# POOL issues later loads, and eight early heads make their scores from split parts

## The chip, the core and the metric

The kernel runs on one core of a Trainium2 chip. The metric is the device time of one execution in microseconds (us): the median of three runs was 1068.83 us, the lowest 1068.21 and the highest 1069.07. The engines are called as in the profile: PE multiplies matrices (PEld is its loading of weights), DVE and ACT work on whole tiles element by element, POOL did little before, and SP only issues transfers.

## What is computed

Eight batches with eight heads of attention over 512 local and 32 global positions, and then a feed-forward layer over all 8 x 544 tokens:

```python
k_all = np.concatenate([k_g, k_l], axis=2)
v_all = np.concatenate([v_g, v_l], axis=2)
s_g = scale * np.matmul(q_g, k_all.transpose(0, 1, 3, 2))
out_g = np.matmul(sm(s_g), v_all)                      # global queries see every key
s_ll = scale * np.matmul(q_l, k_l.transpose(0, 1, 3, 2))
mask = np.abs(pos[:, None] - pos[None, :]) <= 32       # local queries see a band
s_ll = np.where(mask, s_ll, -1000000000.0)
s_lg = scale * np.matmul(q_l, k_g.transpose(0, 1, 3, 2))
a_l = sm(np.concatenate([s_lg, s_ll], axis=-1))
out_l = np.matmul(a_l, np.concatenate([v_g, v_l], axis=2))
x = concat([out_g, out_l], axis=2) as (8*544, 512)
h = np.maximum(x @ w_in, 0.0)                          # (512, 2048)
out = h * h @ w_out                                    # (2048, 512)
```

All inputs and outputs are float32. `sm` is a softmax over the last axis.

## The kernel before

The attention is cut into 128 head slots, `t` = 0 to 127: one head with one half (256) of its local queries. Sixteen slots hold one batch. A slot's keys, queries and values lie in one packed tile `raw` of 128 x 864 (columns 0 to 351 keys, 352 to 607 queries, the rest values), and keys and queries stand there twice, in partitions 0 to 63 and 64 to 127. The feed-forward layer works on blocks of 256 tokens; a block takes eight steps `m`, each with 256 of the 2048 inner columns. One program loop has a step `t` for every slot, and in it the feed-forward step `m = t - 9` (`LAG`).

Precision is bought in two ways. The first sixteen slots (`plain`, `NPLAIN` = 16) multiply float32 tiles as they are, and with keys and queries there twice their scores come out twice as large (`scale` is 0.0625 then). Every later slot is split (`split_head`, lines 125 to 137): ACT copies `raw` into `hi` in the format fp32r, DVE subtracts to get the rest, `lo`, and in the lower half of `hi` the keys are replaced by their own rests. `scores` (line 139) then makes each half of a slot's scores from two products, `hi` with `hi` and `lo` with `hi`, instead of one float32 product. The global queries' scores, `g_scores` (line 287), run against `qz`, a zeroed float32 tile that POOL fills for plain slots (lines 273 to 278), or against `qgz`, which holds the split queries, for the others; four slots share one. `g_evac` (line 301) takes the sums `gs` to `sg`: for split slots it is a copy on ACT and an addition on DVE.

Around this run the softmax (`softmax1` on DVE, `softmax2` on ACT, `softmax3` on DVE or ACT), the transposes of the probabilities into `pt`, their copy `pts` by ACT, the product with the values into `xa`, and its copy by ACT into `xg` or `x_h`. The weights come as 32 chunks `wr`, which ACT (`w_abs`) and DVE (`w_bits`, two operations) turn into float32 chunks `wf` for the first block; one such turn of a chunk is called a decode below. Later ACT and DVE make the split chunks `ws` from them (`w_chunk`). The table `PLAN` says at which of four places of step `t` a half decode (`b`) or a split (`s`) is written; what the table leaves out is made when it is needed (`w_need`).

For steps before 17 (`FREE`) the order of each engine's instructions is set by a scheduler from its own estimates; from step 17 on PE, DVE and ACT keep the order in which the program is written. All loads and stores but the first global query stand in SP's queue.

Of the kernel before, what the change touches and what calls it, by code (L numbers as in the profile page):

```python
# [16 lines left out]
P = 128  # L17
# [10 lines left out]
NPLAIN = 16  # L28

PLAN = [",,,b", "b,,,b", "b,,,b", "b,,b,", "b,,b,", "b,,b,", "b,,b,", "b,b,,b", "b,b,,b", "bb,bb,bb,bb", "bb,bb,bb,bb", "bbs,bb,bbs,bbs", "bbs,bbs,bbs,bbs", "bbs,bbs,bbs,bbs", "bbs,bbs,bs,s", "ss,s,s,s", "ss,s,s,s", "s,,s,", "s,,s,", "s,,s,", "s,,s,", "s,,s,", "s,,s,"]  # L30
# [28 lines left out]
def attention_moe(  # L59
# [10 lines left out]
    pe, ve, ac = InOrder(tc, nc.tensor), InOrder(tc, nc.vector), InOrder(tc, nc.scalar)  # L70
    PSUM = bass.MemoryType.PSUM
# [18 lines left out]
    def load_head(t):  # L90
# [5 lines left out]
        if t == 0:  # L96
            nc.sync.dma_start(raw[:, : QC + KC], pk[t, :, : QC + KC])
        else:
            nc.sync.dma_start(raw, pk[t])
# [165 lines left out]
    def g_load(t):  # L265
# [7 lines left out]
        if plain(t):  # L273
            qz = p1.tile([P, 512], F32, tag=("ph", "gvl", "gvh", "ph")[t // 4], name=f"qz{t}")
            nc.gpsimd.memset(qz, 0.0)
            qr = p1.tile([P, 2, 2, 32], F32, tag="qr", name=f"qr{t}")
            (nc.sync if t else nc.scalar).dma_start(qr, src)
            nc.gpsimd.tensor_copy(cols(qz, 0), qr)
# [8 lines left out]
    def g_scores(t):  # L287
# [4 lines left out]
        kk = hd["raw" if plain(t) else "hi"]  # L292
# [35 lines left out]
    def g_soft(t):  # L328
# [260 lines left out]
    for t in range(NSTEP + LAG + 1):  # L589
# [40 lines left out]
        if early and t + 1 < NPLAIN:  # L630
            scores(t + 1)
# [11 lines left out]
        if t + 1 < NT:  # L643
            split_head(t + 1)
# [126 lines left out]
```

## Time and profile before

| | before |
|---|---|
| median of 3 runs | 1068.83 us |
| the profiled execution's own time | 1068.82 us |
| its span | 1067.0 us |
| busy: PE, DVE, ACT, POOL | 1050.4, 856.3, 753.1, 3.9 us |
| granted clock of PE | 1.00 |
| DMA, read and written | 86.51 and 8.91 MB |

The span is what the instructions take from the first to the last; 1.8 us lie around it. Rows of the timeline give the start, the length and the engine of a group of equal instructions, and in brackets the idle time before it with what ended it. Rows of the stretches give, after the bounds and the length, the busy time of PE, PEld, DVE, ACT and POOL with the number of instructions in brackets, the granted clock, the share of the DMA engines and GB/s. Rows of the groups end with the total busy time and the mean length of one instruction in ns.

### The profile page before, as it was taken

Reading aid. Unit: us, or ns where it says so; the run is one execution under the profiler, and the core shown is the slowest. Engines: PE = TensorE matmul, PEld = TensorE weight load, DVE = VectorE, ACT = ScalarE, POOL = GpSimd, SP = SyncE. Lnnn points to the kernel's source line nnn. Section 1 sums busy time; section 2 is a strip of 40 time slices with the busy share of each in tenths; the row PEclk is TensorE's granted clock in tenths of the full one; section 3 lists DMA queues with packets and bytes.
Section 4 is the critical chain, followed back from the end, with each engine's and each line's share of the span. In section 5 each row is a group of like instructions: output and inputs, shape, how many; then the busy total and the mean of one; then the engine's idle time right before and its main releaser. Section 6 shows DMA issues by size and latency. Waiting matters only on the chain.

```text
span 1067.0 us, 21142 instructions
## 1 busy us (share of the span) xinstructions
PE 1050.4 (98%) x7568; PEld 941.7 (88%) x7568; DVE 856.3 (80%) x2687; ACT 753.1 (71%) x1901; POOL 3.9 (0%) x14
## 2 busy tenths in 40 slices
PE   7999999999999999999999999999999999999998
PEld 6776889999998989998999989999999989999896
DVE  5698988898888989988888888888888888874321
ACT  5898877778777776778777777777777787774322
POOL 1000000000000000000000000000000000000000
PEclk9999999999999999999999999999999999999999
DMA  9772132223222322222322222223221322201000
GB/s 372 310 263 74 57 106 76 71 80 98 68 89 64 103 65 83 74 91 77 94 71 82 86 72 76 90 66 100 78 89 55 94 86 66 88 29 33 13 20 20
DMA packets 54312, 96.78 MB, mean 91 GB/s; under 512 B 4288, under 2 KB 29376, under 8 KB 54208
## 3 DMA queue, kind: packets, MB, share of 16 engines
q1 hardware_dynamic: 54064, 95.37, 27.2%
q8 instruction: 60, 0.98, 0.4%
q14 instruction: 44, 0.36, 0.1%
q10 hardware_dynamic: 144, 0.07, 0.0%
HBM read 86.51 MB, written 8.91 MB: 89 GB/s over the span
## 4 chain that ended last, share of the span: by engine, by line
PE 87%; ACT 7%; DVE 4%; issue 1%; DMA 0%; ACTq 0%
PE o L52 33%; PE h L52 32%; PE xa L52 7%; PE s L52 6%; PE pt L52 5%; PE gxo L52 2%; PE gs L52 2%; ACT prob L52 1%; DVE prob L52 1%; ACT r L52 1%; ACT ph L52 1%; ACT hi L52 1%; ACT ot L52 1%; PE gt L52 1%; ACT sg L52 0%
## 5 line engine op out<-in xcount | busy, mean ns | idle before, releaser
L52 PE MATMUL h<-x_h,ws 128*128 128x256 f32 x2048 | 388.9, 283 | 0.0
L52 PEld LDWEIGHTS h<-x_h,ws 128*128 128x128 f32 x2048 | 327.0, 191 | 0.5
L52 PE MATMUL o<-ws,gh 128*128 128x512 f32 x1024 | 321.3, 395 | 0.0
L52 PE MATMUL h<-x_l,ws 128*128 128x256 f32 x1024 | 289.1, 282 | 0.1
L52 PEld LDWEIGHTS o<-ws,gh 128*128 128x128 f32 x1024 | 185.5, 188 | 34.6
L52 PE MATMUL o<-ws,gl 128*128 128x512 f32 x512 | 202.6, 396 | 0.0
L52 PEld LDWEIGHTS h<-x_l,ws 128*128 128x128 f32 x1024 | 195.9, 191 | 0.9 <-DVE x_l L52 0.4
L52 ACT CAST ph<-pt 128x256 fp32r<-128x256 f32 x448 | 141.1, 341 | 67.7 <-PE pt L52 60.8
L52 ACT ACTIVATE prob<-prob,st 128x224 f32<-128x224 f32 x270 | 127.8, 475 | 61.2 <-DVE st L52 59.1
L52 ACT ACTIVATE r<-h 128x512 f32<-128x512 f32 x136 | 81.4, 599 | 112.3 <-PE h L52 112.3
L52 PEld LDWEIGHTS o<-ws,gl 128*128 128x128 f32 x512 | 96.2, 188 | 22.7
L52 DVE CUSTOM_DVE_ANT_0 prob<-s,con 128x224 f32<-128x224 f32 x256 | 90.0, 386 | 24.5 <-PE s L52 23.2
L52 DVE TENSOR_TENSOR gl<-r,gh 128x512 fp32r<-128x512 f32 x128 | 87.9, 686 | 23.3 <-ACT gh L52 20.5
L52 ACT CAST hi<-raw 128x864 fp32r<-128x864 f32 x112 | 102.5, 915 | 1.4
L52 DVE TENSOR_TENSOR r<-h,r 128x512 f32<-128x512 f32 x82 | 56.7, 692 | 51.9 <-ACT r L52 50.6
L52 PE MATMUL xa<-ph,hi 128*64 128x128 f32 x448 | 87.3, 238 | 1.6 <-DVE ph L52 1.2
L52 DVE TENSOR_TENSOR hi<-raw,hi 64x352 fp32r<-64x352 f32 x224 | 82.5, 368 | 6.4
L52 ACT CAST gh<-r 128x512 fp32r<-128x512 f32 x128 | 79.1, 618 | 9.1 <-DVE r L52 8.7
L52 DVE TENSOR_TENSOR ph<-pt,ph 64x128 fp32r<-64x128 f32 x224 | 79.6, 355 | 7.0
L52 DVE TENSOR_TENSOR lo<-raw,hi 128x448 fp32r<-128x448 f32 x112 | 69.6, 622 | 15.3 <-ACT hi L52 12.5
L52 PE MATMUL pt<-con,prob 128*128 128x128 f32 (+1 forms) x512 | 78.2, 274 | 0.7 <-ACT prob L52 0.5
L52 DVE TENSOR_SCALAR prob<-prob,st 128x224 f32<-128x224 f32 x242 | 70.7, 334 | 4.1
(80 smaller groups left out, 1572.7 us busy)
## 6 DMA issues: line engine op xcount, KB each, us to landing
raw<-in_pk_dram SPq DMA_DIRECT2D x127, 432.0 KB, 3.2
wr<-in_w_dram SPq DMA_DIRECT2D x32, 512.0 KB, 7.9
gv<-in_vg_dram SPq DMA_DIRECT2D x32, 320.0 KB, 3.3
out_dram<-ot SPq DMA_DIRECT2D x32, 256.0 KB, 2.2
qr<-in_qg_dram SPq DMA_DIRECT2D x31, 64.0 KB, 2.8
out_dram<-ot SPq DMA_DIRECT2D x8, 64.0 KB, 1.7
con<-in_consts_dram SPq DMA_DIRECT2D x2, 224.0 KB, 5.1
raw<-in_pk_dram SPq DMA_DIRECT2D x1, 304.0 KB, 3.2
```

Source lines behind the costliest of these rows:

```text
L52: r = method(*args, **kwargs)
```

## The change

Three things are changed. First, POOL issues every load of a slot from 16 on, every load of global values (`gv`) and every load of global queries that are split (`qr`), in program order (`po`); POOL's memsets and copies now keep that order too. Second, slots 4 to 11 (`SCORES`) make their scores and their global scores from split parts: ACT copies 608 columns (keys and queries) to `hi`, DVE makes a `lo` of 256 columns and replaces the lower half's keys. Their values and probabilities stay plain. Slots 0 to 3 and 12 to 15 are as before (`whole`), but `g_evac` halves their global sums, so that one scale of 0.125 serves all. Third, `PLAN` writes the splits of the weights otherwise in steps 17 to 23: one fewer in each of steps 17 to 22 but 18, which has none, and two in step 23. For the sixteen early slots the split of the next slot is now written directly ahead of its scores.

```diff
+SCORES = range(4, 12)
-PLAN = [",,,b", "b,,,b", "b,,,b", "b,,b,", "b,,b,", "b,,b,", "b,,b,", "b,b,,b", "b,b,,b", "bb,bb,bb,bb", "bb,bb,bb,bb", "bbs,bb,bbs,bbs", "bbs,bbs,bbs,bbs", "bbs,bbs,bbs,bbs", "bbs,bbs,bs,s", "ss,s,s,s", "ss,s,s,s", "s,,s,", "s,,s,", "s,,s,", "s,,s,", "s,,s,", "s,,s,"]
+PLAN = [",,,b", "b,,,b", "b,,,b", "b,,b,", "b,,b,", "b,,b,", "b,,b,", "b,b,,b", "b,b,,b", "bb,bb,bb,bb", "bb,bb,bb,bb", "bbs,bb,bbs,bbs", "bbs,bbs,bbs,bbs", "bbs,bbs,bbs,bbs", "bbs,bbs,bs,s", "ss,s,s,s", "ss,s,s,s", "s,,,", ",,,", "s,,,", "s,,,", "s,,,", "s,,,", "s,,s,"]
...
+    po = InOrder(tc, nc.gpsimd)
...
+    def whole(t):
+        return plain(t) and t not in SCORES
...
-            nc.sync.dma_start(raw, pk[t])
+            (nc.sync if plain(t) else po).dma_start(raw, pk[t])
...
-        if plain(t):
+        if whole(t):
             return
         hi = p2.tile([P, PK], F32R, tag="hi", name=f"hi{t}")
         lo = p2.tile([P, QC + 192], F32R, tag="lo", name=f"lo{t}")
-        ac.copy(hi, raw)
-        ve.tensor_sub(lo, raw[:, KC : KC + QC + 192], f(hi[:, KC : KC + QC + 192]))
+        e = KC + QC if plain(t) else PK
+        n = min(e - KC, QC + 192)
+        ac.copy(hi[:, :e], raw[:, :e])
+        ve.tensor_sub(lo[:, :n], raw[:, KC : KC + n], f(hi[:, KC : KC + n]))
         ve.tensor_sub(hi[64:, :KC], raw[64:, :KC], f(hi[64:, :KC]))
-        ve.tensor_sub(hi[32:64, PK - 64 :], raw[32:64, PK - 64 :], f(hi[32:64, PK - 64 :]))
+        if not plain(t):
+            ve.tensor_sub(hi[32:64, PK - 64 :], raw[32:64, PK - 64 :], f(hi[32:64, PK - 64 :]))
...
-            if plain(t):
+            if whole(t):
                 pe.matmul(s[:, u, :], hd["raw"][:, qs], hd["raw"][:, ks], start=True, stop=True)
             else:
                 pe.matmul(s[:, u, :], hd["hi"][:, qs], hd["hi"][:, ks], start=True, stop=False)
                 pe.matmul(s[:, u, :], hd["lo"][:, u * P : u * P + P], hd["hi"][:, ks], start=False, stop=True)
...
-        if plain(t):
+        if whole(t):
             qz = p1.tile([P, 512], F32, tag=("ph", "gvl", "gvh", "ph")[t // 4], name=f"qz{t}")
-            nc.gpsimd.memset(qz, 0.0)
+            po.memset(qz, 0.0)
...
-            nc.gpsimd.tensor_copy(cols(qz, 0), qr)
+            po.tensor_copy(cols(qz, 0), qr)
         else:
             qz = qgz
             qr = p1.tile([P, 2, 2, 32], F32, tag="qr", name=f"qr{t}")
-            nc.sync.dma_start(qr, src)
+            po.dma_start(qr, src)
             ac.copy(cols(qgz, 0), qr)
             ve.tensor_sub(cols(qgz, 1), qr, f(cols(qgz, 0)))
...
-            ac.copy(dst, gs[:64, cols] if early else gs[64:, cols])
+            if early:
+                ac.activation(out=dst, in_=gs[:64, cols], func=AF.Copy, scale=0.5)
+            else:
+                ac.copy(dst, gs[64:, cols])
...
-        nc.sync.dma_start(gv, src.rearrange("(c p) n -> p c n", p=P))
+        po.dma_start(gv, src.rearrange("(c p) n -> p c n", p=P))
...
         if early and t + 1 < NPLAIN:
+            split_head(t + 1)
             scores(t + 1)
...
-        if t + 1 < NT:
+        if NPLAIN <= t + 1 < NT:
             split_head(t + 1)
```

The table moves instructions by the scheduler as well. Three places matter. The number before the underscore in a name is the slot, the step or the chunk (`pts9` is the copy of slot 9's transposed probabilities, `wr6` chunk 6 of the weights, `o0` the feed-forward output's first half); the number behind it only tells buffers apart.

The first place is ACT between the copies of slots 8 and 9. Before:

```order
L52 COPY pts8_430<-pt_95 128x512
L52 ACTIVATE prob1_94<-prob1_94,st9_432 128x224
L52 ACTIVATE wf4_262<-wr5_260 128x512
L52 COPY sg_91<-gs6_331 64x288
L52 ACTIVATE r0_456<-h0_425 128x512
L52 ACTIVATE r0_456<-r0_456 128x512
L52 ACTIVATE wf6_329<-wr6_294 128x512
L52 CAST x_h_88<-xa8_449 64x256
L52 COPY pts9_492<-pt_95 128x512
```

Now:

```order
L53 COPY pts8_472<-pt_95 128x512
L53 ACTIVATE wf6_350<-wr7_348 128x512
L53 ACTIVATE prob1_94,st9_474<-prob1_94,st9_474 128x224 x2
L53 ACTIVATE r0_505<-h0_467 128x512
L53 ACTIVATE prob1_94<-prob1_94,st9_474 128x224
L53 ACTIVATE wf8_422<-wr8_389 128x512
L53 ACTIVATE r0_505<-r0_505 128x512
L53 CAST x_h_88<-xa8_491 64x256
L53 ACTIVATE prob1_94<-prob1_94,st9_474 128x224
L53 ACTIVATE wf8_422<-wr9_420 128x512
L53 COPY pts9_543<-pt_95 128x512
```

The copy of slot 9 stood behind the decode of chunk 6 and stands behind that of chunk 9 now: three decodes have moved ahead of it. All eight new copies to `hi` stand ahead of this place too.

The second place is PE around the values' product of slot 9. Before:

```order
L52 MATMUL pt_95<-con_78,prob1_94 96x128 x2
L52 MATMUL h1_487<-xg_90,wf4_262 128x256 x8
L52 MATMUL xa9_512<-pts9_492,raw9_140 128x256
L52 MATMUL xa9_512<-pts9_492,raw9_140 128x128 x2
L52 MATMUL s11_516<-raw11_207 128x224 x2
L52 MATMUL o0_0_533<-wf2_190,r0_456 128x512
L52 MATMUL gs8_402<-raw8_122,qz8_379 128x288
L52 MATMUL gs8_402<-raw9_140,qz8_379 128x288
L52 MATMUL o1_0_534<-wf2_190,r0_456 128x512
L52 MATMUL gs10_506<-raw10_173,qz8_379 128x288
```

Now:

```order
L53 MATMUL pt_95<-con_78,prob1_94 96x128 x2
L53 MATMUL gs10_557<-hi10_495,qgz_92 128x288
L53 MATMUL h1_538<-xg_90,wf4_268 128x256 x4
L53 MATMUL xa9_563<-pts9_543,raw9_140 128x256
L53 MATMUL xa9_563<-pts9_543,raw9_140 128x128 x2
L53 MATMUL s11_572<-hi11_567 128x224
L53 MATMUL s11_572<-hi11_567,lo11_568 128x224
L53 MATMUL s11_572<-hi11_567 128x224
L53 MATMUL s11_572<-hi11_567,lo11_568 128x224
L53 MATMUL o0_0_591<-wf2_190,r0_505 128x512
L53 MATMUL o1_0_592<-wf2_190,r0_505 128x512
```

The global scores of slots 8, 9 and 10 stood behind `xa9` and are done ahead of it now; of `h1` four products stand directly ahead of it where eight stood.

The third place is POOL's queue behind its first memsets. Before:

```order
L275 MEMSET qz0_99 128x512
L275 MEMSET qz4_239 128x512
L275 MEMSET qz8_379 128x512
L278 COPY qz0_99<-qr0_101 128x2x2x32
L275 MEMSET qz12_604 128x512
L278 COPY qz4_239<-qr4_241 128x2x2x32
```

Now:

```order
L53 MEMSET qz0_99 128x512
L53 COPY qz0_99<-qr0_101 128x2x2x32
L53 DMA qr4_246<-in_qg_dram 128x128
L53 DMA qr8_415<-in_qg_dram 128x128
L53 MEMSET qz12_664 128x512
L53 COPY qz12_664<-qr12_666 128x2x2x32
L53 DMA gv11_0_669<-in_vg_dram 128x5x128
L53 DMA raw16_863<-in_pk_dram 128x864
```

Two of the four zeroed tiles are gone, and the queries of slots 4 and 8 are loaded from this queue as soon as the copy ahead of them is done. On ACT the conversion of `qr4` is now the first instruction behind the loading of its table.

More of the change, by code (lines that the diff above doesn't have):

```diff
@@ L120, in attention_moe @@
     pt = ps_a.tile([P, 512], F32, name="pt")
-    nc.gpsimd.memset(f(qgz), 0.0)
-    nc.gpsimd.memset(sg[:, :, 608:], 0.0)
+    po.memset(f(qgz), 0.0)
+    po.memset(sg[:, :, 608:], 0.0)
     nc.vector.memset(pt[96:, 256:], 0.0)
@@ L152, in scale @@
     def scale(t):
-        return 0.0625 if plain(t) else 0.125
+        return 0.0625 if whole(t) else 0.125
     def softmax1(t):
@@ L291, in g_scores @@
             state["gs"] = ps_a.tile([P, 416], F32, tag="gs", name=f"gs{t}")
-        kk = hd["raw" if plain(t) else "hi"]
+        kk = hd["raw" if whole(t) else "hi"]
         pe.matmul(
@@ L303, in g_evac @@
         gs = state["gs"]
-        early = plain(t)
+        early = whole(t)
         parts = ((0, 0, 288),) if (t // 8) % 2 == 0 else ((288, 0, 160), (448, 192, 96))
@@ L331, in g_soft @@
         ve.tensor_reduce(out=st[:, 0:1], in_=s[:, :544], op=ALU.max, axis=AX.X)
-        ve.tensor_scalar(out=st[:, 1:2], in0=st[:, 0:1], scalar1=-scale(t), scalar2=None, op0=ALU.mult)
+        ve.tensor_scalar(out=st[:, 1:2], in0=st[:, 0:1], scalar1=-0.125, scalar2=None, op0=ALU.mult)
         state["gst", t] = st
@@ L336, in g_exp @@
         s, st = sg[:, (t // 4) % 2, :544], state["gst", t]
-        ac.activation(out=s, in_=s, func=AF.Exp, scale=scale(t), bias=st[:, 1:2], accum_out=st[:, 2:3])
+        ac.activation(out=s, in_=s, func=AF.Exp, scale=0.125, bias=st[:, 1:2], accum_out=st[:, 2:3])
     def g_norm(t):
```

## The prediction

> **What bounds the kernel now.** I read the totals first, then stretches of time, then the timelines of single engines up to 60 us. The totals say that PE is nearly never idle:
>
> ```profile
> PE 1050.4 (98%) x7568; PEld 941.7 (88%) x7568; DVE 856.3 (80%) x2687; ACT 753.1 (71%) x1901; POOL 3.9 (0%) x14
> ```
>
> That is an average, so I took stretches (bounds and length, then PE, PEld, DVE, ACT and POOL):
>
> ```profile
> 5.90:20.00 14.10, 12.20 (x63) 10.15 (x63) 9.22 (x46) 9.96 (x31) 0.53 (x1) 1.00 1.03 414
> 20.00:40.00 20.00, 18.84 (x108) 15.66 (x107) 13.12 (x58) 16.14 (x44) 0.88 (x3) 1.00 1.01 392
> 40.00:44.70 4.70, 4.70 (x25) 4.27 (x25) 2.67 (x10) 3.46 (x10) 0.00 (x0) 1.00 1.02 413
> 6.87:39.60 32.73, 29.68 (x165) 24.82 (x165) 21.07 (x98) 25.70 (x73) 1.41 (x4) 1.00 1.02 401
> 40.00:60.00 20.00, 20.00 (x86) 14.69 (x86) 16.07 (x50) 17.05 (x44) 0.00 (x0) 1.00 0.47 181
> 60.00:80.00 20.00, 20.00 (x89) 14.86 (x88) 18.20 (x48) 18.10 (x43) 0.00 (x0) 1.00 0.90 328
> 80.00:100.00 20.00, 19.55 (x93) 13.77 (x92) 18.02 (x41) 18.87 (x42) 0.00 (x0) 1.00 0.17 60
> 500.00:600.00 100.00, 99.79 (x758) 91.26 (x757) 87.62 (x277) 73.15 (x191) 0.00 (x0) 1.00 0.25 77
> ```
>
> From 40 us on PE does its own work without a pause, and whatever is taken from it comes off the end, if the others follow. Up to 100 us they follow only just: ACT is busy for 54.0 of the 60 us from 40 to 100 (90%), in its densest 20 us for 18.87 (94%), and DVE for up to 18.20 (91%). Ahead of 40 us the softmax of the first ten slots on ACT and DVE sets the pace, and PE has pauses. So the change is a trade in the first 50 us: less PE work against more ACT and DVE work where those two have little room.
>
> **PE's own saving.** What a group costs PE is the distance from its start to the next start, since lengths overlap:
>
> ```profile
> 38.21 0.92 PE L52 MATMUL s<-raw 128*128 128x224 f32 x4
> 38.97 0.60 PE L52 MATMUL pt<-con,prob 128*128 128x128 f32 x4
> ...
> 42.86 1.04 PE L52 MATMUL xa<-pts,raw 128*128 128x256 f32 x6
> ...
> 47.18 0.65 PE L52 MATMUL gs<-raw,qz 128*128 128x288 f32 x2
> 47.67 1.88 PE L52 MATMUL o<-wf,r 128*128 128x512 f32 x4
> ...
> 400.99 0.35 PE L52 MATMUL s<-hi 128*128 128x224 f32 x1
> ...
> 401.51 0.29 PE L52 MATMUL h<-x_h,ws 128*128 128x256 f32 x1
> ...
> 404.98 0.30 PE L52 MATMUL gs<-hi,qgz 128*128 128x288 f32 x1
> 405.12 0.62 PE L52 MATMUL o<-ws,gh 128*128 128x512 f32 x2
> ```
>
> A plain slot's scores take 38.97 - 38.21 = 0.76 us, a split slot's, though twice the products, 401.51 - 400.99 = 0.52. A plain global score takes 47.67 - 47.18 = 0.49, a split one 405.12 - 404.98 = 0.14. Eight slots save 8 x (0.24 + 0.35) = **4.7 us of PE work**.
>
> **What ACT and DVE get for it.** The prices:
>
> ```profile
> L52 ACT CAST hi<-raw 128x864 fp32r<-128x864 f32 x112 | 102.5, 915 | 1.4
> L52 ACT CAST qgz<-qr 128x128 fp32r<-128x128 f32 x28 | 8.4, 299 | 0.7
> L52 ACT ACTIVATE wf<-wr 128x512 f32<-128x512 f32 x32 | 21.6, 674 | 0.2
> L52 ACT COPY sg<-gs 64x160 f32<-64x160 f32 x32 | 9.2, 288 | 1.6 <-PE gs L52 0.7
> L52 DVE TENSOR_TENSOR pl<-pt,ph 128x256 fp32r<-128x256 f32 x112 | 47.1, 421 | 2.8 <-ACT ph L52 1.9
> L52 DVE TENSOR_TENSOR hi<-raw,hi 64x352 fp32r<-64x352 f32 x112 | 58.5, 522 | 3.2
> L52 DVE TENSOR_TENSOR sg<-gs,sg 64x288 f32<-64x288 f32 x28 | 12.6, 450 | 0.9
> L52 DVE TENSOR_TENSOR sg<-gs,sg 64x160 f32<-64x160 f32 x28 | 8.9, 317 | 0.8
> L52 DVE TENSOR_SCALAR wf<-wf 128x512 int32<-128x512 int32 x32 | 13.5, 422 | 3.4 <-ACT wf L52 3.3
> L52 DVE SCALAR_TENSOR_TENSOR wf<-wr,wf 128x512 int32<-128x512 int32 x32 | 22.0, 688 | 0.5
> ```
>
> A copy of 608 columns lies between 864 (0.915) and 128 (0.299); by their slope it takes 0.70. In a dense stretch two casts of 0.623 take 1.12 together, the last row of the next fence, so each start comes some 0.12 ahead of the last end; I take that off every added instruction, as busy time is counted once. ACT gets, ahead of the copy of slot 9's transposes (the first place of the change): eight copies to `hi`, 8 x 0.58 = 4.6; two casts of `qgz`, 0.4; two more `sg` copies, 0.3; and three decodes that were behind it, 3 x 0.55 = 1.7. Together **7.0 us**. DVE gets, ahead of slot 10's first softmax row: eight `lo` (256 columns, as in `pl`), 8 x 0.34 = 2.7 at 0.08 off; eight `hi`, 8 x 0.44 = 3.5; four additions to `sg`, 1.2; two for `qgz`, 0.4; three decodes, 3 x 0.95 = 2.9. Together **10.7 us**. The decodes are borrowed: they are gone from the stretch behind.
>
> How much room is there? The markers (starts and lengths):
>
> ```profile
> 6.87 0.48 ACT L52 ACTIVATE prob<-prob,st 128x224 f32<-128x224 f32 x1 [4.42 <-DVE st L52]
> 9.32 0.48 ACT L52 ACTIVATE prob<-prob,st 128x224 f32<-128x224 f32 x1 [1.42 <-DVE st L52]
> 39.60 0.59 ACT L52 COPY pts<-pt 128x512 f32<-128x512 f32 x1
> 80.53 1.12 ACT L52 CAST ws<-wf 128x512 fp32r<-128x512 f32 x2
> 44.70 0.39 DVE L52 CUSTOM_DVE_ANT_0 prob<-s,con 128x224 f32<-128x224 f32 x1 [1.87 <-PE s L52]
> ```
>
> From its first exponential at 6.87 to slot 9's copy at 39.60 ACT is busy for 25.70 of 32.73 us. With 7.0 more it has 32.7 to do. Without any pause the copy starts at 39.6 and ends at 40.2; at the densest share of this trace (94%) 32.7 / 0.94 = 34.8, and it ends at 42.3; at 90% at 43.8; at the share of 20 to 40 us (81%) at 47.8. The product `xa9` waits for it and started at 42.86, since eight products of `h1` stood ahead of it. PE's own work ahead of `xa9` shrinks by 2.7 (seven scores, 1.7; four global scores, 1.4; less the three that move ahead of it, 0.4). So `xa9` moves by -2.7 (PE alone), -0.6 (ACT at 94%), +0.9 (at 90%) or +4.9 (at 81%). DVE says about the same: 9.22 + 13.12 + 2.67 = 25.0 busy of 38.8 from 5.90 to 44.70; 35.7 at 91% are 39.2, so +0.4, and with none of the 0.08 taken off (28 instructions, 2.2) 37.9 / 0.91, +2.9. I take **+0.9** for `xa9`: both engines have to be dense at once, and each waits for the other, so the mean of 40 to 100 us is nearer than its best part, while the decodes moved ahead give both something to do in their pauses.
>
> Behind `xa9` PE has 2.1 us less (three global scores of 0.49 already done, 0.35 for that of slot 11, 0.24 for its scores), and ACT and DVE have three decodes less. **-2.1** counts in full, as PE has no pause there. Two later pauses may shrink:
>
> ```profile
> 98.23 0.55 PE L52 MATMUL pt<-con,prob 128*128 128x128 f32 x3 [0.45 <-ACT prob L52]
> ...
> 124.20 0.34 PE L52 MATMUL s<-hi 128*128 128x224 f32 x1 [0.66 <-DVE hi L52]
> ```
>
> Steps 17 to 22 lose a weight split each on ACT and DVE, and nothing is then forced at once: the second half of chunks is wanted only up to step 25, one by one. Of these 1.1 us I count **-0.3**, because up to step 16 ACT and DVE still have every weight split that they had, and it is there that the first of the two arises.
>
> **The move to POOL's queue.** SP's own waits cost nothing where PE never waits for a load, and a load takes its time wherever it is issued. No row shows a load by POOL. The nearest ones:
>
> ```profile
> 3.81 0.29 POOL L278 COPY qz<-qr 128x128 f32<-128x128 f32 x1 [1.08 <-DMA qr<-in_qg_dram]
> ...
> 400.83 0.33 SPq L99 DMA_DIRECT2D raw<-in_pk_dram  x1
> ...
> 413.74 0.92 ACT L52 CAST hi<-raw 128x864 fp32r<-128x864 f32 x1
> raw<-in_pk_dram SPq DMA_DIRECT2D x127, 432.0 KB, 3.2
> ```
>
> A later slot's load is issued when its buffer comes free (400.83) and read two steps later (413.74): it has 12.9 us and takes 3.2 from SP. POOL's order holds `gv` and `qr` loads between the slots' loads, but each waits only for a step already past. So I cost it at **zero**, under the cover of 9.7 us. The Trainium skill speaks against this half of the change: "SBUF — State Buffer", section "SBUF: two separate sides", says that descriptors of loads issued by POOL are written by POOL itself, and that DVE's two-port copies lock it out meanwhile. It gives a load of 0.62 us alone and 3.1 beside such a copy; added to 3.2 that would be, as an estimate, 5.7 us, still under 12.9.
>
> One load by POOL does stand on the path: `qr4`, whose conversion is ACT's first instruction now. POOL can issue it when its copy at 3.81 is done, at 4.1. The first `qr`, from ACT's queue, landed by 3.81 at the latest, so a like load lands at 6.8 to 7.9, and the first exponential starts up to 1.3 us late; up to 1.4 is covered by ACT's pause ahead of slot 1's, the 1.42 in the row at 9.32 above. I count **+0.2**, and +1 at the upper end.
>
> **Sum.** +0.9 - 2.1 - 0.3 + 0.2 = -1.3. The profiled execution's span goes from 1067.0 to 1065.7 us; 1.8 us lie around it, and its time is that of the median. Forecast **1067.5 us**: no change that can be told, which for this kernel means within 0.2% (1066.7 to 1071.0).
>
> **Rivals.**
> 1. *PE stays the bound from the start.* If ACT runs at 94% or better up to slot 9, `xa9` moves by -0.6 to -2.7, and half or all of the two pauses go: -0.6 - 2.1 - 0.6 = -3.3 to -2.7 - 2.1 - 1.1 = -5.9, so 1065.5 to 1062.9. For it: decodes are written between the new copies. Against it: 94% was reached only where nobody waited for ACT.
> 2. *ACT and DVE become the bound for ten slots* (slower). If ACT keeps the share it has now from 20 to 40 us, `xa9` moves by +4.9 and the end by +4.9 - 2.1 + 0.2 = +3.0; with the head late by 1 us, +3.8: 1071.8 to 1072.6. It decides once ACT is under 82% busy up to slot 9 (32.7 / 0.82 = 39.9, `xa9` at 47.4, +4.5). For it: DVE's new subtractions stand in front of the softmax rows of the same slots, and are on their path; against it, that stretch was less dense because PE's products came late there, and these get cheaper.
> 3. *POOL's loads come late or hold DVE up* (slower). Each slot would have to take over 12.9 us to land. Or DVE is held: it has 12.4 us free in the 100 us from 500 to 600, in which 12 to 13 slots are loaded (two steps are the 12.9 us above and the 2 to 3 until the buffer is free), so some 1.0 per load; what is beyond costs 112 times, and 1.1 us a load would give +11, 1080. The skill's rule above is this mechanism; no row here has both engines at it.
> 4. *The queue does nothing* is part of the forecast: its term is zero.
>
> **Chances and range.** Forecast 0.40, rival 1 0.35, rival 2 0.18, rival 3 0.07. Rival 1 is faster by over 0.2%, the last two are slower: faster 0.35, same 0.40, slower 0.25. The forecast's own range is 1066.5 to 1070.5. For eight in ten I go from the low end of rival 1 to the upper one of rival 2: 1063.0 to 1073.0.
>
> **What would show it.** `xa9` within 42 to 45 us, ACT around 90% and DVE around 91% busy from 7 to 43 us, PE's pauses ahead of 45 us up from 3 to about 6 or 7; score groups of 0.52 and global ones of 0.14 in slots 4 to 11; from 150 us on each step as before, and no wait of ACT for `raw`. Wrong: `xa9` beyond 47 or ahead of 41.5; a first exponential after 8.5; a PE busy share under 99% from 500 to 600; or a loss behind `xa9`, where ACT has to reach slots 13 and 14.

## The result, and the profile after

The changed kernel takes 1093.17 us (median of 4 runs, 1092.36 to 1094.60) against 1068.82 us in the runs beside it: a ratio of 1.0228, 95% interval 1.0213 to 1.0243, or **24.4 us slower**. The forecast was 1067.5, its range 1063.0 to 1073.0. The profiled execution, the slowest of the four, took 1094.6 us with a span of 1092.8.

The page's totals and the stretches of the changed kernel (bounds and length, then PE, PEld, DVE, ACT, POOL, the granted clock, DMA):

```profile
PE 1059.0 (97%) x7560; PEld 947.0 (87%) x7560; DVE 866.1 (79%) x2711; ACT 757.5 (69%) x1911; POOL 107.1 (10%) x184
```

```profile
5.90:20.00 14.10, 9.63 (x36) 7.92 (x34) 6.18 (x32) 7.17 (x20) 0.83 (x2) 0.76 1.02 412
20.00:40.00 20.00, 13.85 (x77) 10.64 (x78) 17.23 (x67) 17.28 (x46) 0.24 (x1) 0.97 0.76 299
...
130.00:160.00 30.00, 25.49 (x173) 22.36 (x172) 21.72 (x70) 19.99 (x49) 2.28 (x5) 0.89 0.22 73
160.00:200.00 40.00, 36.27 (x257) 32.58 (x256) 31.22 (x97) 25.64 (x67) 3.98 (x7) 0.91 0.25 77
500.00:600.00 100.00, 99.83 (x753) 91.18 (x752) 88.00 (x278) 74.11 (x191) 11.23 (x19) 1.00 0.26 81
...
11.50:18.30 6.80, 4.57 (x16) 3.95 (x17) 3.81 (x16) 4.37 (x15) 0.55 (x1) 0.50 1.03 416
38.80:42.20 3.40, 3.40 (x12) 2.84 (x11) 3.34 (x13) 1.60 (x4) 1.70 (x3) 0.50 0.65 211
93.40:96.80 3.40, 3.40 (x9) 2.65 (x8) 3.17 (x8) 1.44 (x4) 0.00 (x0) 0.50 0.00 0
151.40:158.20 6.80, 5.23 (x18) 4.25 (x19) 5.87 (x19) 5.09 (x11) 0.00 (x0) 0.50 0.00 0
188.90:195.80 6.90, 5.42 (x19) 4.33 (x20) 6.50 (x22) 4.94 (x13) 0.54 (x1) 0.51 0.22 64
```

The same two later stretches of the kernel before:

```profile
130.00:160.00 30.00, 29.29 (x221) 26.30 (x220) 26.62 (x81) 22.76 (x58) 0.00 (x0) 1.00 0.31 96
160.00:200.00 40.00, 40.00 (x303) 36.68 (x302) 35.51 (x110) 28.91 (x75) 0.00 (x0) 1.00 0.24 76
```

Three things are seen. From 500 to 600 us nothing has changed: PE is busy for 99.83 of 100 us. PE lacks work ahead of 40 us (9.63 of 14.10 where it had 12.20) and again from 130 to 200 us (61.8 of 70, before 69.3). And in five stretches, 27.3 us together, PE's clock is granted at half; before, it was 1.00 throughout the rows shown.

To put the loss in its place I use one mark per step, the start of the ReLU that ACT makes of the feed-forward sums (`r` from `h`). From step 17 on PE, DVE and ACT follow the program's order, so the marks can be compared directly; ahead of that the scheduler may place the ReLU a little differently. The changed kernel's marks, less those of before:

| step (start before, us) | 9 (37.5) | 14 (83.1) | 17 (110.9) | 19 (128.1) | 21 (145.5) | 25 (175.5) | 28 (197.3) | 144 (1056.2) |
|---|---|---|---|---|---|---|---|---|
| later by, us | 11.3 | 13.6 | 13.0 | 12.3 | 18.2 | 25.2 | 25.2 | 25.9 |

So **12.3 us are lost up to step 19, 12.9 from there to step 25, and 0.7 in the 880 us behind.** The rows at both places, first ACT's timeline (start, length, in brackets the idle time and its end):

```profile
10.36 1.28 ACT L53 ACT_TABLE_LOAD   x1 [10.36 <-DMA qr<-in_qg_dram]
11.65 0.30 ACT L53 CAST qgz<-qr 128x128 fp32r<-128x128 f32 x1
11.86 0.48 ACT L53 ACTIVATE prob<-prob,st 128x224 f32<-128x224 f32 x1
...
148.43 0.30 ACT L53 CAST qgz<-qr 128x128 fp32r<-128x128 f32 x1 [5.34 <-DMA qr<-in_qg_dram]
...
187.44 0.30 ACT L53 CAST qgz<-qr 128x128 fp32r<-128x128 f32 x1 [5.96 <-DMA qr<-in_qg_dram]
```

then POOL's, whose rows are now mostly issues of loads:

```profile
4.10 0.29 POOL L53 COPY qz<-qr 128x128 f32<-128x128 f32 x1 [2.29 <-DMA qr<-in_qg_dram]
4.70 0.68 POOL L53 DMA_DIRECT2D qr<-in_qg_dram  x1 [0.30 <-POOL qz L53]
...
137.33 0.57 POOL L53 DMA_DIRECT2D raw<-in_pk_dram  x1 [7.37 <-ACT ph L53]
144.65 0.54 POOL L53 DMA_DIRECT2D raw<-in_pk_dram  x1 [6.75 <-DVE sg L53]
145.18 0.54 POOL L53 DMA_DIRECT2D qr<-in_qg_dram  x1
159.35 0.54 POOL L53 DMA_DIRECT2D raw<-in_pk_dram  x1 [13.64 <-DVE hi L53]
```

and PE's:

```profile
13.73 1.15 PE L53 MATMUL pt<-con,prob 128*128 128x128 f32 x4 [4.34 <-DVE prob L53]
...
150.72 0.24 PE L53 MATMUL xa<-ph,hi 128*64 128x128 f32 x1 [2.45 <-DVE ptl L53]
152.97 0.37 PE L53 MATMUL xa<-pl,hi 128*64 128x128 f32 x1 [1.94 <-DVE pl L53]
```

Each time ACT stands at the conversion of a split query load `qr`. At the head this conversion is the very first thing in ACT's order. At step 19 the load was issued at 145.18, and only because the load ahead of it in POOL's order, that of slot 21, had been waiting for a buffer until 144.65; its conversion was due right then. In the kernel before, the same `qr` had been issued long ahead, at 61.42, and the one behind it at 132.66 as soon as the buffer was read (SP's timeline):

```profile
61.42 0.33 SPq L282 DMA_DIRECT2D qr<-in_qg_dram  x1
...
132.66 0.33 SPq L282 DMA_DIRECT2D qr<-in_qg_dram  x1
```

The stretches at half clock begin in or behind PE's pauses: the first, at 11.45, in the pause of 4.34 us that ends at 13.73; the fourth, at 151.40, behind the pause of 2.45 us and in that of 1.94. From step 19 to 25 the two parts add up. PE's idle time from 130 to 200 us grew from 0.7 to 8.2 us, which is 7.5, and the products that filled 5.23 + 5.42 = 10.65 us at half clock would have taken half of that at the full clock, some 5.3 less by estimate. Together 12.8, against 12.9 by the marks. The Trainium skill, "TensorE: Matmul & The Clock Gate", Part 1, says that the clock falls to half after an idle window of about 3.4 us and is given back after a busy one; the stretches here are 3.4 or 6.8 us long and at 0.50, which agrees. An idle window wasn't needed here, though: in the 3.4 us ahead of the second stretch (35.35 to 38.76 us) PE was busy for 1.65 us, and its longest pause there was 1.13.

### The profile page after: what moved, and what is told of

Read it like the earlier page. It is cut to its first block, busy times and chain, and to the rows that moved or that the text cites. A ratio compares the mean times of both kernels' runs of the same rounds, so it can differ in the third digit from the quotient of the medians.

```text
span 1092.8 us, 21147 instructions
## 1 busy us (share of the span) xinstructions
PE 1059.0 (97%) x7560; PEld 947.0 (87%) x7560; DVE 866.1 (79%) x2711; ACT 757.5 (69%) x1911; POOL 107.1 (10%) x184
## 4 chain that ended last, share of the span: by engine, by line
PE 80%; ACT 9%; DVE 6%; DMA 2%; issue 1%; SPq 0%; POOL 0%; ACTq 0%; DVEq 0%; POOLq 0%
PE o L53 31%; PE h L53 30%; PE xa L53 6%; PE s L53 5%; PE pt L53 4%; PE gxo L53 2%; DVE prob L53 2%; ACT prob L53 2%; PE gs L53 2%; DMA qr<-in_qg_dram 1%; ACT r L53 1%; DVE wf L53 1%; ACT ph L53 1%; DMA wr<-in_w_dram 1%; ACT hi L53 1%
## 5 line engine op out<-in xcount | busy, mean ns | idle before, releaser
L53 POOL DMA_DIRECT2D raw<-in_pk_dram x112 | 61.0, 545 | 725.6 <-DVE hi L53 321.4
L53 DVE CUSTOM_DVE_ANT_0 prob<-s,con 128x224 f32<-128x224 f32 x256 | 90.0, 386 | 27.3 <-PE s L53 26.2
L53 ACT CAST hi<-raw 128x864 fp32r<-128x864 f32 (+1 forms) x120 | 107.9, 900 | 1.3
L53 DVE TENSOR_TENSOR hi<-raw,hi 64x352 fp32r<-64x352 f32 x232 | 86.7, 374 | 6.7
L53 DVE TENSOR_TENSOR lo<-raw,hi 128x448 fp32r<-128x448 f32 (+1 forms) x120 | 73.1, 610 | 15.7 <-ACT hi L53 13.0
```

Of the source, the lines that this page charges most:

```text
L53: r = method(*args, **kwargs)
```

## The experiments

The kernels and their times; each ratio is to the kernel before, run beside it.

| | what | median, us | ratio (95%) |
|---|---|---|---|
| r1 | changed kernel, old `PLAN` | 1087.70 | 1.0174 (1.0159 to 1.0189) |
| r2 | changed kernel, split `qr` by SP | 1082.25 | 1.0127 (1.0111 to 1.0142) |
| r3 | changed kernel without split slots | 1080.66 | 1.0114 (1.0097 to 1.0131) |
| r4 | split slots alone | 1083.21 | 1.0133 (1.0118 to 1.0148) |
| r6 | POOL's queue alone | 1074.98 | 1.0058 (1.0041 to 1.0075) |
| r10 | r3 with `qr` three steps ahead | 1068.17 | 0.9994 (0.9985 to 1.0003) |
| r9 | r4 with `qr4` at the start | 1077.99 | 1.0086 (1.0071 to 1.0101) |
| r12 | r4 with more `hi` buffers | 1075.83 | 1.0066 (1.0051 to 1.0082) |
| r13 | r9 and r12 together | 1075.90 | 1.0065 (1.0049 to 1.0082) |
| r20 | before, with splits that nobody reads | 1070.31 | 1.0011 (1.0001 to 1.0020) |
| r24 | r4, but only the local scores split | 1075.52 | 1.0063 (1.0048 to 1.0078) |
| r21 | r13, splits one slot earlier | 1076.04 | 1.0067 (1.0050 to 1.0084) |
| r16 | r4 with slots 8 to 11 only | 1072.36 | 1.0030 (1.0019 to 1.0041) |
| r22 | changed kernel, `qr4` at the start | 1085.65 | 1.0157 (1.0142 to 1.0172) |
| r14 | changed kernel, all three remedies | 1074.55 | 1.0049 (1.0034 to 1.0064) |
| r18 | r10 with slots 12 to 15 split | 1072.93 | 1.0039 (1.0024 to 1.0054) |

The marks of the steps, less those of the kernel before (us):

| step | 9 | 14 | 17 | 19 | 21 | 25 | 144 |
|---|---|---|---|---|---|---|---|
| changed | 11.3 | 13.6 | 13.0 | 12.3 | 18.2 | 25.2 | 25.9 |
| r1 | 11.4 | 13.7 | 13.1 | 13.1 | 18.9 | 19.0 | 19.6 |
| r2 | 12.9 | 12.6 | 11.5 | 10.8 | 10.4 | 12.5 | 13.1 |
| r3 | -0.3 | 0.3 | -0.4 | -1.1 | 4.5 | 11.2 | 11.0 |
| r4 | 12.6 | 14.5 | 13.9 | 14.0 | 13.9 | 14.0 | 14.6 |
| r6 | 0.1 | 0.7 | 0.0 | -0.1 | 6.0 | 6.0 | 6.2 |
| r10 | 0.0 | -0.6 | -0.6 | -1.3 | -1.7 | 0.0 | -0.3 |
| r9 | 6.6 | 8.2 | 8.4 | 8.4 | 8.4 | 8.4 | 9.0 |
| r12 | 6.5 | 6.8 | 6.1 | 6.1 | 6.1 | 6.1 | 7.0 |
| r13 | 4.5 | 5.4 | 5.5 | 5.5 | 5.5 | 5.5 | 6.4 |
| r20 | 2.1 | 2.7 | 0.8 | 0.8 | 0.8 | 0.9 | 1.5 |
| r24 | 4.5 | 6.9 | 6.1 | 6.1 | 6.1 | 6.2 | 6.7 |
| r21 | 6.6 | 7.2 | 6.5 | 6.5 | 6.5 | 6.5 | 7.5 |
| r16 | 1.7 | 4.9 | 3.0 | 3.0 | 3.0 | 3.0 | 3.7 |
| r22 | 6.3 | 5.6 | 4.8 | 4.1 | 9.0 | 15.5 | 16.1 |
| r14 | 5.6 | 5.2 | 4.1 | 3.4 | 3.0 | 4.7 | 5.7 |
| r18 | 0.6 | 3.1 | 2.7 | 2.0 | 1.6 | 3.3 | 4.3 |

### The parts apart: r1 to r4

Theory A: all of the loss comes from the order in which POOL issues. r1 puts the table of before back into the changed kernel. r2 changes one line of it:

```diff
-            po.dma_start(qr, src)
+            nc.sync.dma_start(qr, src)
```

r3 takes the split slots out of it:

```diff
-SCORES = range(4, 12)
+SCORES = range(0)
```

r4 is the split slots alone, against the changed kernel:

```diff
-PLAN = [... the new table]
+PLAN = [... the table of before]
-    po = InOrder(tc, nc.gpsimd)
+    po = nc.gpsimd
-            (nc.sync if plain(t) else po).dma_start(raw, pk[t])
+            nc.sync.dma_start(raw, pk[t])
-            po.dma_start(qr, src)
+            nc.sync.dma_start(qr, src)
-        po.dma_start(gv, src.rearrange("(c p) n -> p c n", p=P))
+        nc.sync.dma_start(gv, src.rearrange("(c p) n -> p c n", p=P))
```

> The changed kernel with the table PLAN of the kernel before; nothing else differs. Theory A (the table keeps the decoded chunk wf31 longer in one of the two raw buffers, so slots' loads wait one behind the other in POOL's order, and the qr loads of steps 19 and 23 behind them): both ACT waits for qr near 148 and 187 us go, and with them the 12.9 us that the changed kernel loses between steps 19 and 25: 1093.2 - 12.9 = 1080, range 1078 to 1083. Theory B (a load by POOL is late whatever stands ahead of it): the waits of 5.3 and 6.0 us stay, 1091 to 1095. The head (first exponential at 11.86 us) is not touched by either.

> The changed kernel with the split query loads (qr) issued from SP's queue instead of POOL's; slots 16 on and gv stay on POOL, PLAN is the new one. Theory A (qr is late because POOL issues it in program order behind other work: its own copy at the head, a slot's load that waits at steps 19 and 23): first exponential back at 6.9 us, no ACT wait for qr near 148 and 187: 12.9 us less there and 5 to 11 less in the first ten slots, 1069 to 1075. Theory C (the split scores overfill ACT and DVE in the first ten slots, and qr4 only hides that): 12.9 less behind step 19, but the ReLU of step 9 stays near 48 us (37.5 before): 1079 to 1081.

> The changed kernel without its split slots (SCORES empty, all 16 plain heads whole as before); POOL's queue and the new PLAN stay. Theory A: the head's 11.3 us and the 2.0 at step 14 are gone, the waits for qr behind step 19 stay (12.9): about 1068.8 + 12.9 = 1081.7, range 1078 to 1084. Theory C (the split slots are what costs, the queue and the table nothing): within 2 us of before, 1067 to 1071.

> The kernel before with the split slots 4 to 11 alone: all loads in SP's queue, PLAN of before. The prediction's own sum without the head: 1068.8 + 0.9 - 2.1 = 1067.6 (1065 to 1070), first exponential at 6.9 us, xa9 at 42 to 45 us. Theory C: xa9 beyond 47 us, 1072 to 1082.

**Measured.** r3 came as theory A said (1080.66; 5.6 lost between steps 19 and 21, 6.7 more up to 25), and with r4 it makes the whole: 11.9 + 14.4 = 26.3 against 24.4. But r4 fell on the other side: the split slots alone cost 14.4 us, 1.2 more than even theory C allowed, nearly all ahead of step 17, with a first exponential at 6.98. r2, slower than both of its theories said (1082.25), has its first exponential back, at 6.74, and lost 12.9 us up to step 9 all the same. So the late head isn't the only way to lose in the front, and theory A holds only for the part behind step 19. r1 gained 5.5 where theory A gave 10 to 15: with the old table the wait at step 23 is gone (19.0 at step 25), the one at step 19 stays.

### The queue: r6 and r10

r6 is the changed kernel with `SCORES` empty and the old table. r10 is r3 with the load of a split `qr` taken out of `g_load` and issued three steps ahead:

```diff
...
+    def g_fetch(t, engine, tag):
+        qr = p1.tile([P, 2, 2, 32], F32, tag=tag, name=f"qr{t}")
+        engine.dma_start(qr, qg[t // 16, (t // 4) % 2].rearrange("p (a b) n -> p a b n", a=2))
+        state["qr", t] = qr
...
+        if t % 4 == 1 and NPLAIN <= t + 3 < NT:
+            g_fetch(t + 3, po, "qr")
```

> The kernel before with POOL's queue alone (slots 16 on, gv and the split qr by POOL in program order; no split slots, PLAN of before). Theory A (qr20 stands in POOL's order behind the load of slot 21, which waits for the splits of slot 20, since the decoded chunk wf31 still holds the other raw buffer): one wait of ACT for qr of about 5 us near step 19, none at step 23: +4.5 + 1.1 as in the run without split slots, and nothing else: 1068.8 + 5.7 = 1074.5 (1073 to 1076.5). Theory B (every load by POOL costs): loss spread over all slots, or over 8 us.

> POOL's queue and the new PLAN without split slots (1080.7), but each qr of slots 16 on is issued three steps ahead of its conversion, in front of the load of a slot in POOL's order. Theory A: both ACT waits for qr (steps 19 and 23) go; the loads of slots stay as late as the one buffer makes them: 1080.7 - 10 = 1069 to 1072. Theory B: under 3 us gained.

**Measured.** r6 came as theory A said: 1074.98, with 6.1 us between steps 19 and 21 and nothing else. r10 gained more than theory A's 9 to 12 us, 12.5: 1068.17, not to be told from the kernel before. So the queue's whole loss is a `qr` load held up behind a slot's load. The order of events: the decoded chunk `wf31` lives in one of the two `raw` buffers until its split `ws31`; until then a slot's load waits for the splits of the slot just before it, and what POOL has to issue behind it waits along. With the old table `ws31` is made in step 20, so one `qr` (step 19) is caught; the new table makes it in step 23, and a second is caught. The loads themselves are hardly slower from POOL's queue (the page's issues, KB each and median us to landing; from SP it was 3.2):

```profile
raw<-in_pk_dram POOLq DMA_DIRECT2D x112, 432.0 KB, 3.5
```

### The front: r9, r12, r13 and r20

In r4 the transposes of slot 5 start at 25.91, those of slot 6 at 40.39. PE's, ACT's and SP's timelines there:

```profile
25.91 0.79 PE L53 MATMUL pt<-con,prob 128*128 128x128 f32 x4 [0.57 <-DVE prob L53]
...
31.43 0.53 PE L53 MATMUL gs<-hi,qgz 128*128 128x288 f32 x2 [2.86 <-DVE qgz L53]
33.72 0.53 PE L53 MATMUL s<-hi 128*128 128x224 f32 x1 [1.76 <-ACT hi L53]
...
40.39 0.33 PE L53 MATMUL pt<-con,prob 128*128 128x128 f32 x1 [0.29 <-DVE prob L53]
```

```profile
29.00 1.22 ACT L53 ACTIVATE wf<-wr 128x512 f32<-128x512 f32 x2
30.11 0.29 ACT L53 CAST qgz<-qr 128x128 fp32r<-128x128 f32 x1
31.87 0.70 ACT L53 CAST hi<-raw 128x608 fp32r<-128x608 f32 x1 [1.47 <-PE gs L53]
```

```profile
16.67 0.33 SPq L290 DMA_DIRECT2D qr<-in_qg_dram  x1
```

SP issues `qr4` at 16.67, the scheduler places its conversion behind two decodes at 30.11, the global scores of slots 4 and 5 wait for it, and the cast of slot 6 waits for them, since only two `hi` buffers exist and slots 4 and 5 hold both (theory D, a ring). r9 opens it at one end (`qr4` gets the buffer of `xs`, free until slot 16, and is issued from ACT's queue at the start), r12 at the other:

```diff
+    g_fetch(4, nc.scalar, "xs")            # r9
...
-        hi = p2.tile([P, PK], F32R, tag="hi", name=f"hi{t}")
+        if plain(t) and t % 4 >= 2 and t < 10:   # r12
+            hi = p1.tile([P, 640], F32R, tag=("gvh", "pth")[t % 2], name=f"hi{t}")
+        else:
+            hi = p2.tile([P, PK], F32R, tag="hi", name=f"hi{t}")
```

r13 has both (and `t < 12`). r20 is the kernel before with `split_head` run for slots 4 to 11, while their scores, global ones too, are still made from the whole tiles.

> The split slots alone (SP's queue, PLAN of before), but qr4 is loaded at the start from ACT's queue into a buffer of its own (that of xs, free until slot 16). Theory D (the stall of 14 us between the transposes of slots 5 and 6 is a ring: the two hi buffers hold slots 4 and 5 until their global scores are done, these wait for qgz, and that for qr4 and its place in ACT's order): the stall goes, transposes keep 3.0 to 3.3 us a slot, the ReLU of step 9 comes at 38 to 41 us (50.1 without the early load): 1083.2 - 9 to 12 = 1071 to 1074. Theory C (ACT and DVE are overfull whatever comes early): under 4 us gained, 1079 to 1083.

> The split slots alone as in r4, qr4 late as there, but slots 6 and 7 take their hi from buffers that are free until step 13 (those of gvh and pth), so four slots can be split ahead. Theory D: hi6 no longer waits for the global scores of slot 4, the scores of 6 and 7 go on, and most of the 14 us stall goes though qr4 is as late as before: 1083.2 - 7 to 11 = 1072 to 1076. If qgz alone holds PE up (its global scores stand in PE's order ahead of the rest): under 3 us gained.

> The split slots alone with both remedies: qr4 loaded at the start into its own buffer, and slots 6, 7, 10 and 11 with their hi in other buffers. Theory D alone (the ring and the late qr4 are all of the loss): 1068 to 1071. Theory C' (what is left after the ring is the work of the splits on ACT and DVE, which stretches each slot from 2.8 to about 4 us): no better than the better of the two single remedies less 2: 1073 to 1077.

> The kernel before (SP's queue, PLAN of before), with the splits of slots 4 to 11 made but read by nobody: ACT's cast of 608 columns and DVE's two subtractions run, the scores are still made from the whole parts. PE's work, qr and the global scores are those of before, and there is no ring. Theory C' (the added work alone stretches the slots): ReLU of step 9 at 41 to 44 us, 1072 to 1077. Theory D: it fits into the idle time of ACT and DVE, ReLU of step 9 within 1 us of 37.5, 1068 to 1070.

**Measured.** The ring is real: r12 gains 7.4 us with `qr4` as late as before, and the jump of 14 us is gone. r9 gained 5.2, between the two theories, and both remedies together no more than r12 alone: 6.9 us stay, where theory C' had put r13. r20 gave 1070.3, 0.3 us above theory D's range and 1.7 below the 1072 to 1077 of "work alone": the eight casts and sixteen subtractions cost 1.3 us when nobody waits for them. Yet they fill both engines, as r20's stretches show:

```profile
15.00:20.00 5.00, 4.29 (x26) 3.39 (x25) 4.92 (x20) 4.83 (x12) 0.00 (x0) 1.00 1.03 418
20.00:25.00 5.00, 5.00 (x29) 3.89 (x29) 4.82 (x23) 4.80 (x16) 0.00 (x0) 1.00 1.03 410
25.00:30.00 5.00, 3.70 (x20) 2.49 (x19) 4.89 (x19) 4.95 (x14) 0.29 (x1) 1.00 1.03 411
```

DVE is busy for 14.63 of these 15 us and ACT for 14.58, 97%. So the two engines can be packed that densely in this stretch, and theory C' (the work alone) doesn't hold. What costs then has to come with somebody waiting for the work.

### Who waits: r24, r21 and r16

r24 is r4 with `plain(t)` in place of `whole(t)` in `g_load`, `g_scores` and `g_evac`: only the local scores are split, and no `qgz` is needed. r21 is r13 with

```diff
-            split_head(t + 1)
+            if t + 2 < NPLAIN:
+                split_head(t + 2)
             scores(t + 1)
```

and r16 is r4 with `SCORES = range(8, 12)`.

> The split slots alone (SP's queue, PLAN of before), but only their local scores are made from split parts; the global scores stay whole (qz and raw), so there is no qgz, no second sg part, and hi is free once the local scores are done: no ring. Local way (the scores wait for ACT's cast and DVE's two subtractions, and the softmax behind them): PE waits for hi and prob stay, 1073 to 1077. Global way (qgz, sg and their place on ACT and DVE are what is left): 1069 to 1071.5, near the 1070.3 of the splits that nobody reads.

> The split slots alone with both remedies (1075.9), and each slot split one slot earlier (two ahead of its transposes instead of one). Local way: PE no longer waits for DVE's hi (2.1 us up to 50 us) and the loss falls by 2 to 5: 1071 to 1074. Global way, or DVE full anyway (97% of 15 to 35 us with the splits alone): within 1 us of 1075.9.

> The split slots alone, but only slots 8 to 11 (4 to 7 whole again; SP's queue, PLAN of before). Their splits fall between 30 and 60 us. Theory C' (work on ACT and DVE): four casts and eight subtractions less, loss 2 to 5 us, 1071 to 1074. By the prediction's sum (from 40 us on PE's saving counts in full): 4 x 0.59 = 2.4 us less PE work, most of it behind xa9: 1066 to 1068.5.

**Measured.** r24 loses 7.0 us, as much as r13 (6.9), which has the split global scores too: the local scores by themselves are enough for the rest of the loss. One slot shows how. In r20, PE and DVE, slot 5:

```profile
17.32 0.92 PE L53 MATMUL s<-raw 128*128 128x224 f32 x4
```

```profile
20.12 0.38 DVE L53 CUSTOM_DVE_ANT_0 prob<-s,con 128x224 f32<-128x224 f32 x1
```

and in r24:

```profile
20.25 0.54 PE L53 MATMUL s<-hi 128*128 128x224 f32 x1
...
22.23 0.35 PE L53 MATMUL s<-hi 128*128 128x224 f32 x1
```

```profile
18.25 0.42 DVE L53 TENSOR_TENSOR lo<-raw,hi 128x256 fp32r<-128x256 f32 x1
18.69 0.52 DVE L53 TENSOR_TENSOR hi<-raw,hi 64x352 fp32r<-64x352 f32 x1
...
23.14 0.38 DVE L53 CUSTOM_DVE_ANT_0 prob<-s,con 128x224 f32<-128x224 f32 x1
```

The subtractions of slot 5 stand at the same place in both (18.25 here, 18.79 there), behind the softmax rows of slot 4 on DVE. Where nobody waits for them, PE has made the scores at 17.32, ahead of them, and DVE goes on with slot 5's rows at 20.12. Where the scores need them, PE makes these at 20.25 and 22.23, and the rows come at 23.14, 3.0 us later. The wait for the subtractions is only a part of these 3.0 us: they end at 19.21 (18.69 and 0.52), and the scores at 20.25 follow other products of PE without a pause. The other part is PE's clock. r24's stretches and a row of PE, then the same row of r20:

```profile
15.00:20.00 5.00, 3.24 (x14) 2.57 (x14) 4.91 (x19) 3.89 (x9) 0.00 (x0) 0.74 1.03 418
20.00:25.00 5.00, 3.96 (x22) 3.14 (x21) 2.68 (x12) 3.86 (x12) 0.09 (x1) 0.91 1.03 413
...
17.67 2.07 PE L53 MATMUL xa<-pts,raw 128*128 128x256 f32 x6 [0.73 <-ACT pts L53]
```

```profile
18.21 1.14 PE L53 MATMUL xa<-pts,raw 128*128 128x256 f32 x6
```

r24 is granted half the clock from 17.44 to 20.85, after pauses of PE of only 0.77, 0.25 and 0.73 us, and the six products take 2.07 us there where r20's take 1.14; r20 has pauses of 0.46 and 0.25 us at this place and keeps the full clock. PE is busy for 3.18 us of the stretch, so by halving some 1.6 of r24's 7.0 us are the slow clock (an estimate). r9, r12, r13 and r14 have one such stretch each ahead of 33 us; r4 has three, with 11.95 busy us, so some 6.0 of its 14.4; r20, r16 and r18 have none (the last 4 us of each run left aside).

Splitting a slot earlier (r21) brought nothing, 1076.04 against 1075.90: up to 50 us PE's waits for `hi` fell from 2.1 us to 1.0, but there are two stretches at half clock instead of one. Why the gain and the loss cancel isn't shown; DVE was not full in r21, 13.07 of the 15 us from 15 to 30 (87%). r16 came in the range of theory C' (1072.36), and against the prediction's counting: half the split slots, the later ones, still lose 3.3 us.

### The changed kernel with the remedies: r22 and r14

r22 is the changed kernel with r9's early `qr4` alone. r14 has the early `qr4`, the `hi` buffers of r13 and r10's `qr` ahead.

> The changed kernel with qr4 alone loaded at the start into its own buffer, so that ACT's first instruction has its data; queue, PLAN and the two hi buffers are unchanged. First exponential at 7.2 us instead of 11.86. If the 5 us of the head go straight to the end: 1093.2 - 4 to 6 = 1087 to 1089, ReLU of step 9 at 43 to 45 us. If the ring or the split work takes it back (as with qr by SP, where the front was 12.9 us late in spite of an exponential at 6.74): 1091 to 1094.

> The changed kernel (split slots, POOL's queue, new PLAN) with all three remedies: qr of slots 16 on three steps ahead, qr4 at the start into its own buffer, hi of four slots in other buffers. If the causes add: what the split slots with both remedies give, less the 0.7 us that queue and PLAN gave with qr ahead: 1072 to 1077, with no ACT wait for qr anywhere. If POOL's queue costs something in the front that these remedies don't reach: 1078 or more.

**Measured.** r22 gains 7.5 us, more than the 5 us of the head. Its first exponential (ACT's timeline):

```profile
5.29 1.28 ACT L53 ACT_TABLE_LOAD   x1 [5.29 <-DMA qr<-in_qg_dram]
6.58 0.30 ACT L53 CAST qgz<-qr 128x128 fp32r<-128x128 f32 x1
7.35 0.48 ACT L53 ACTIVATE prob<-prob,st 128x224 f32<-128x224 f32 x1 [0.47 <-DVE st L53]
```

The head is 4.5 us earlier, and with PE's pause of 4.34 us the stretches at half clock up to 100 us are gone as well (11.37 busy us by the rows of the changed kernel, so some 5.7 us by halving). r14 lands at 1074.55, 5.5 us above before, with no wait of ACT for `qr` from 130 us on. So the 24.4 us of the changed kernel are accounted for: 7.5 for the late `qr4`; 5.5 that stay; the rest, 11.4, between r22 and r14, mostly for the two `qr` waits behind step 19 (between steps 19 and 25 r22 loses 11.4 by its marks and r14 1.3). The added `hi` buffers count for little here: at step 17 r22 is 4.8 us late and r14 4.1. So the ring that cost r4 so much is no large part of the changed kernel's loss.

### Where PE had no pause: r18

r18 is r10 with `SCORES = range(12, 16)`.

> POOL's queue with qr ahead and the new PLAN (1068.2), and split slots 12 to 15 instead of 4 to 11: these lie between 63 and 105 us, where PE had no pause before. By the prediction's way of counting: 4 x 0.59 = 2.4 us less PE work, and the end 2.4 us earlier: 1065.8, range 1064.5 to 1067. If ACT, 94% busy from 80 to 100 us, takes it back: 1068 to 1072.

**Measured.** 1072.93, 4.8 us slower than r10, where the counting gave 2.4 faster. r18 from 70 to 80 us, then r10, then before:

```profile
70.00:80.00 10.00, 7.21 (x33) 4.68 (x32) 9.92 (x29) 9.71 (x23) 0.00 (x0) 1.00 0.51 159
```

```profile
70.00:80.00 10.00, 10.00 (x46) 7.33 (x46) 9.29 (x23) 9.49 (x22) 0.00 (x0) 1.00 0.63 202
```

```profile
70.00:80.00 10.00, 10.00 (x46) 7.46 (x45) 9.90 (x26) 9.90 (x28) 0.00 (x0) 1.00 0.85 305
```

PE was fully busy there before, but so were DVE and ACT, 9.90 of 10 us each; in r10, which differs from r18 in one line, they were busy for 9.29 and 9.49. In r18 PE waits for DVE, 2.79 us for `x_l` ahead of 79.37 and 1.69 us for `pth` ahead of 84.42. So here the work added to DVE and ACT came out of PE; that no other order would have had room for it isn't shown. No version tried is faster than the kernel before.

## Why the prediction was wrong, point by point

- **"So I cost it at zero, under the cover of 9.7 us"** (POOL's queue): wrong by about 12 us, the largest miss. The cover was read from two rows at 400 and 413 us and taken for the whole run. Between 100 and 190 us one of the two `raw` buffers holds `wf31`: a slot's load is then read as little as 4.0 us after its issue (168.04, ACT's cast at 172.06), which just suffices, and a `qr` behind such a load has no cover at all. The sentence that failed is "POOL's order holds `gv` and `qr` loads between the slots' loads, but each waits only for a step already past": the load of slot 21 waits for the splits of slot 20, which belong to the same step as the `qr` behind it. SP's queue had the same loads, but in the scheduler's order, with `qr` far ahead. r6 and r10 show it.
- **"I count +0.2, and +1 at the upper end"** (`qr4` on the head): it measured 7.5 (r22). The estimate let it be issued at 4.1 and land at 6.8 to 7.9; it was issued at 4.70, ACT got it at 10.36, and ACT's table load, 1.28 us, which began at 1.17 in the kernel before, stood behind the same wait. The 4.34 us in which PE then had nothing to do brought the half clock, which no term held.
- **"I take +0.9 for `xa9`"**: in the changed kernel it starts at 54.33, 11.5 later. As a sum of busy time the term was sound: with the splits made and unread (r20) `xa9` and the end both move by 1.3, and both engines reach 97%. What it left out is order. The scores of a slot now come after work of DVE that stands behind the softmax of the slot ahead, and PE's short pauses ahead of them bring the half clock. With two `hi` buffers and one `qgz` four slots hang together too, but that cost r4 7.4 us and the changed kernel under 1 (r22 to r14). The prediction said "DVE's new subtractions stand in front of the softmax rows of the same slots, and are on their path", as a point for rival 2, but priced rival 2 by ACT's share alone (81%). With every remedy the front still loses 4 to 6 us (r13, r14).
- **"-2.1 counts in full, as PE has no pause there"**: the opposite. r18 and r16 lose where the saving should have counted; in r16 `xa9` moves by 0.9, and step 14 is 4.9 us late. PE without a pause was read as PE alone at its limit; in 70 to 80 us all three engines were at 99% or more, which the 20 us stretches of the prediction (91% for DVE, 94% for ACT) had averaged away.
- **"-0.3" for the two later pauses, and the new table**: small as said, but for another reason. In r10 step 21 is 1.7 us earlier and step 25 is level again, so the table moves work and saves nothing; and "nothing is then forced at once" missed that `wf31` keeps a slot's buffer until its split, which cost the second `qr` wait.
- **The prices of single operations held.** In the changed kernel the cast of 608 columns takes 0.696 us (0.70 forecast) and the `lo` of 256 columns 0.419 (0.421); the four products of a slot's scores start 0.11 to 0.19 us apart.
- **Rivals.** Rival 3 (POOL's loads slow, or DVE held up) is refuted as it was put: loads land in 3.5 us, PE is 99.83% busy from 500 to 600 us, and the 0.6 us lost between steps 28 and 144 appear in r4 too, which has no load by POOL. The Trainium skill's rule of "SBUF — State Buffer", section "SBUF: two separate sides", on POOL's loads beside DVE's two-port copies, weighed there, shows no cost here with DVE busy for 88 of 100 us; how many of DVE's operations are such copies no run shows. Rival 2 had the right place, and its +4.9 for `xa9` is near what r13 and r14 leave with the remedies (47.60 and 48.09, so +4.7 and +5.2); the late `qr4`, the clock and the `qr` waits it did not hold.
- **What was to show it wrong did:** `xa9` beyond 47, a first exponential after 8.5, and a loss behind `xa9`, all three.

What stays open: of the last 5.5 us (r14) some 1.7 are the slow clock, by halving the 3.41 busy us of its one stretch; how much of the rest is the waiting itself and how much the other order that the scheduler chose with it wasn't parted.

## What to carry to other kernels

When a load moves to a queue that keeps program order, look for the longest wait of any load ahead of it, over the whole run and not in its steady part: it inherits that wait, and a buffer that something else borrows for a while is where to look. Time saved on an engine that never pauses counts only if the engines that feed it have room in the same few microseconds, so read their shares in short stretches. Work that is cheap while nobody reads its result can cost several times as much once it stands between one slot's softmax and the next slot's products.

## What the runs showed of the hardware

- PE's clock was granted at half for 3.4 or 6.8 us at a time, five times in the changed kernel up to 1090 us, and no pause as long as that was needed: each stretch begins at the end of 3.4 us in which PE was busy for 0.59 to 1.65 us. In r24 it was 1.89 us (14.03 to 17.44), with no pause over 0.77. Where the limit lies isn't shown. In the 12.9 us lost behind step 19 the slow clock is some 5.3 us, not much less than the pauses' 7.5. A wait of ACT of 5.3 us cost 6.1 at the end (r6).
- A load of 64 KB that POOL issued at 4.70, while the DMA engines were at their full share (1.02), was there only at 10.36, 5.7 us later. The like load that ACT issued at 1.18 (r22) was there at 5.29, 4.1 us later.
- ACT's table load stands in order with the rest: with the conversion of `qr4` as its first instruction it started at 10.36 (5.29 with the early load), not at the start of the program.
